# Weight chunks from 66 on behind the second stage's first rows, the first four chunks one by one, five constant products between the stages

## The chip, the cores and the metric

One core of a Trainium2 chip runs the whole program. The metric is the device time of one execution in microseconds (us). Below, PE is TensorE (matrix products), ACT is ScalarE, DVE is VectorE, POOL is GpSimd and SP is SyncE, which here only issues DMA transfers.

## What is computed

Three layers in a row. An attention with 16 heads, in which a query sees the keys of its own bucket (six sign bits of a projection); a mixture of eight experts, one for each token; and a mixture of eight experts, two for each token.

```
mask = q_bucket[:, :, :, None] == k_bucket[:, :, None, :]
scores = where(mask, scale * q @ k.T, -1e9);  attn = softmax(scores);  x = attn @ v      # 16 heads, 768 x 64
# x: 1536 tokens x 512
for e in range(8):  out[mask_e] = gate_w * (relu(x[mask_e] @ w1[e]) @ w2[e])              # first MoE, top 1
for e in range(8):  out[mask_ke] += top2_w * (relu(x[mask_ke] @ w1[e]) @ w2[e])           # second MoE, top 2
```

## The kernel before

All three layers are one program. The attention is the first stage of a plan; the two mixtures of experts are the second plan, whose experts 0 to 7 are the first MoE and 8 to 15 the second (here "first stage" is the first MoE and "second stage" the second MoE where the experts are spoken of). Each plan is an instance of `Plan` (L98): every step is added with an engine, a length, a due time and the steps that it waits for, and `order()` simulates the engines and takes, among the steps that can start soon, the one that is due first. The result is a fixed order for each engine. The tables `LENGTH`, `SHIFT`, `WAITS` (L36 to L79; with a 2 for the second plan) correct lengths and due times, and so set that order. Each engine then works through its order and waits at semaphores only for what a step reads.

Products are taken in fp32r: each fp32 operand is split into a high and a low part, and three products are added (L1130 to L1132 for the first layer of an expert, m1; L1160 to L1167 for the second). The weights of the 16 experts come in 128 chunks of 512 KB, chunk n = 8 * expert + c, c from 0 to 3 of w1 and from 4 to 7 of w2. `wload` (L246, the DMA is L257) brings a chunk into one of four `wraw` buffers, on SP's queue; `wsplit_h` (L266) makes the high part on ACT, `wsplit_l` (L272) the low part on DVE, for chunks 0 to 3 on POOL. Chunks 64 to 67 are the w1 of the second stage's first expert, chunks 68 to 71 its w2.

In the attention, the bits of a head's buckets are brought into the operand ka by a small DMA on SP, `bits_copy` (L646), and the product of ka and qa (L659) adds the mask to the scores. SP also issues the loads of each head (`loads`, L448 and L449), copies of q and k (L573, L613) and the fills with zeros of the slots in DRAM (`init_x`, L519). Chunks 0 to 3 are loaded in this stage too.

Between the experts, the rows of the second stage go through DRAM. When the first stage's expert e is done, its rows are routed: `rank_start` (L296, L298) and `rank_mm` (L304, L306) count places on PE, DVE turns the count into an index (L319, L322, tile pi), and POOL scatters the rows with four indirect DMAs (`r2_scatter`, L1276) into xs2, the slots of the second stage. `x2_load(0)` (L1306) reads the slots of the second stage's first expert back, tile xr, 104 x 4 x 512 numbers (832 KB). It waits for the scatters of experts 0 to 6. Expert 7's own rows don't take that way: PE adds them by products with one-hot matrices (`y_put`, L1263) to the transposes of the loaded rows (`x8_tr`, L1089, over `slot_start`, L806; 16 transposes), and ACT and DVE split the sum (`x_h`, `x_l`). Ahead of that, `y_h` and `y_l` (L1251, on POOL) split expert 7's result. Constant products of a zero tile wt (`warm`, L239) stand at the program's start.

The number `HOLD` (L94) names the chunk from which on ACT's split waits for the second stage's first rows to be split, and `FIRST2` the chunk whose load waits for `x2_load` to be issued; the loads stand in one line, so all later chunks follow it. The lines of the plan that the change touches are L975 (chunks 0 to 7 in the first plan), L1414 (the loads of the second), L1448 (the transposes) and L1517 (`y_l`).

Of the kernel before, what the change touches and what calls it, by code (L numbers as in the profile page):

```python
# [9 lines left out]
F32 = mybir.dt.float32  # L10
# [8 lines left out]
NB, NHEAD, S, DH = 2, 8, 768, 64  # L19
NBITS = 6  # L20
HEADS = NB * NHEAD
N, D, E, F = NB * S, NHEAD * DH, 8, 1024
# [30 lines left out]
SHIFT = {'c4': -30, 'e0t': 30, 'en1': -80, 'ene': -30, 'ex': -17.2, 'fa': 5.2, 'fo': -140, 'fr': 7, 'fs': -135,  # L53
# [4 lines left out]
WAITS = {'PE': (0, 0.0), 'ACT': (5, 0.0), 'DVE': (265, 0.0), 'POOL': (880, 0.0)}  # L58
LENGTH2 = {('POOL', 'gm', 1742): 2363, ('POOL', 'iw', 1100): 750, ('ACT', 'wh', 520): 521, ('DVE', 'wl', 600): 602, ('Q', 'wr', 2100): (2100, 1500), ('POOL', 'xm', 1023): 783,
# [6 lines left out]
    ('ACT', 'xh', 400): 403, ('DVE', 'xlo', 503): 509, ('ACT', 'xh', 745): 791, ('DVE', 'xlo', 936): 933, ('PE', 'm1', 2276): 2267, ('ACT', 'rh', 745): 761,  # L66
# [3 lines left out]
SHIFT2 = {'g1a': -95, 'g1b6': -15, 'g2a': 10.3, 'g4a': -40, 'g5a': -40, 'g5aa': -150, 'g5b6': -80, 'g9a': 15, 'gia': 20,  # L70
    'gib6': 35, 'gpa': -45, 'gva': 75, 'm1a': -7, 'm1b': 20, 'm1c': 7, 'm2a': -5, 'm2b': 14, 'm2c': 1,
    'rha': 12, 'rhb': -140, 'rla': -25, 'rlb': 25, 'sqa': -15, 'wh0a': -25, 'wh0b': 40, 'wh1a': 2, 'wh1b': -20,
    'wl0a': -35, 'wl0b': -10, 'wl0c': 45, 'wl1a': -5, 'wl1b': 35, 'wr0a': -24, 'wr0b': -18, 'wr1a': -45, 'xha': -60,
    'xhb': -20, 'xla': -25, 'xlb': -50, 'xloc': 85, 'xtb': 35, 'yc0a': -60, 'yca': -63, 'ycb': 20, 'ycc': 105,
    'yra': 5, 'yta': -2}
WAITS2 = {'PE': (0, 0.0), 'ACT': (120, 1.0), 'DVE': (0, 0.18), 'POOL': (120, 0.0)}
WAIT = 120
# [10 lines left out]
RA, K8, L1, L2, RS = 0, 7, 20, 1, 14  # L88
WP, WR, WS = 4, 30, 2.5
# [3 lines left out]
XZ, XSB = 13, 2  # L93
W0, GO, HOLD, FIRST2, WZ = 7, 300, 69, 69, -12  # L94
LONE = 30


class Plan:  # L98
# [8 lines left out]
    def add(self, name, eng, dur, fn, due, deps=(), use=(), new=(), lat=0):  # L107
        t = self.length.get((eng, name[0], dur), dur)
        dur, lat = t if isinstance(t, tuple) else (t, lat)
        due += self.shift.get(self.group(name, eng), 0)  # L110
        self.steps[name] = (eng, dur, fn, due, tuple(deps), tuple(use) + tuple(new), tuple(new), lat)
# [68 lines left out]
def lsh_attention_moe_moe2_kernel(  # L180
# [4 lines left out]
    nc = tc.nc  # L185
# [6 lines left out]
    psp = main.enter_context(tc.tile_pool(name="psp", bufs=1, space=PSUM))  # L192
# [7 lines left out]
    wt = con.tile([128, 128], F32R, name="wt")  # L200
# [285 lines left out]
    for i in range(2):  # L486
        QA.append(acon.tile([128, S], F32R, name=f"qa{i}"))
        a = acon.tile([128, S], F32R, name=f"ka{i}")
# [9 lines left out]
    en = rt.tile([E, D], F32, name="en", bufs=1)  # L498
# [300 lines left out]
    XP, XR, OH = {}, {}, {}  # L799
# [52 lines left out]
    add = plan.add  # L852
# [121 lines left out]
    for c in range(8):  # L974
        add(("wr", c), "SP", 1700, P(wload, c), (WR if c < WP else 222) + c, ([("in", 2)] if c < WP else [("in", len(inits) - 1)]) + ([("wl", c - 4, 7)] if c > 3 else []),  # L975
            lat=2500)
# [104 lines left out]
    def x_turn(key, dp):  # L1081
# [5 lines left out]
        XP[key, 2 * dp, 2] = t  # L1087

    def x8_tr(d, half):  # L1089
        if half == 0:  # L1090
            if d == 0:
                P = psp.tile([128, 2, 512], F32, name="S", bufs=2)
                XP[E, 0], XP[E, 1] = P[:, 0], P[:, 1]
            elif d > 1:
                XP[E, d] = psp.tile([128, 512], F32, name="ET", bufs=3)
        slot_start(XP[E, d], X2[0], range(2 * half, 2 * half + 2), MB, d, True)
# [327 lines left out]
    for key in range(2 * E):  # L1424
# [15 lines left out]
        for dp in range(2):  # L1440
            if key % E:
                add(("xt", key, dp), "DVE", 585 if one else 1004, P(x_turn, key, dp), z - XZ + 2 * dp,
                    [("xl", key)], use=[("xr", key)], new=[("xs", (key, dp))])
        if key == E:
            for d in range(4):
                for h in range(2):
                    k, r = 2 * d + h, [x8(d)]
                    add(("xt", E, k), "PE", 430, P(x8_tr, d, h), z - 13 + k,  # L1448
                        [("xl", E), ("yt", 7, 3) if k < K8 else ("g7", 7)] + [("xt", E, k - 1)] * (k > 0),
                        use=[("xr", E)] + r * (h == 1 or d == 1), new=r * (h == 0 and d != 1))  # L1450
        xp = pieces(key)
# [40 lines left out]
        if one:  # L1492
# [16 lines left out]
            if e == E - 1:  # L1509
                for b in range(2):  # L1510
                    add(("oh", b), "DVE", 480, P(y_ones, b), t - 1, [("g7", e)] + [("oh", 0)] * b,
                        use=[rr, ("O", ("r", e))] + [("hh", "oh")] * b, new=[] if b else [("hh", "oh")])
                    for dp in range(2):
                        y = t - .3 if dp else z + q * 14
                        ob, l = [("yo", "b")], [("ys", (-1, b, dp))]
                        add(("yh", b, dp), "ACT", 358, P(y_h, b, dp), y + .5 + .1 * b, [("yr", e, b, dp), ("yob",)], use=[tt(b, dp), mt] + ob)
                        add(("yl", b, dp), "POOL", 680, P(y_l, b, dp), y + .5 + .1 * b, [("yh", b, dp)], use=ob + [("row", e)], new=l)  # L1517
                        add(("xo", dp, b), "PE", 700, P(y_put, dp, b), t + 1 + dp + .1 * b, [("yl", b, dp), ("oh", b), ("xt", E, 4 * dp + 3)] + [("xo", dp, 0)] * b,
                            use=[x8(2 * dp), x8(2 * dp + 1), ("hh", "oh")] + ob + l)
# [196 lines left out]
```

## Time and profile before

| | |
|---|---|
| median of 3 runs | 778.31 us (776.13 to 780.4) |
| profiled execution | 780.1 us |
| its span in the trace | 778.4 us |
| PE busy | 755.1 us, 97% |
| mean granted clock of PE | 0.985 |

The span runs from the first to the last record of the trace; the profiled execution's own time is 1.7 us longer. All rows below are of this one execution. Times in the trace count from the start of the span. [...] Busy time of PE is counted by records, whatever its clock; PEld are its weight loads, which run beside the products. The DMA share is the mean busy share of the core's 16 DMA engines, GB/s what they moved. In a row of a timeline, the brackets hold the idle time before and what ended it.

### The profile page before, as it was taken

The page shows a single profiled execution, that of the slowest core. Times are in us where ns is not written, and L with a number is a line of the kernel's source. Part 1 is how long each engine was busy: PE and PEld are TensorE (multiplying, and loading weights), DVE is VectorE, ACT ScalarE, POOL GpSimd, SP SyncE. Part 2 cuts the span into 40 slices and gives each one's busy share as a digit, 9 for nine tenths or more (in the row PEclk, how much of TensorE's full clock was granted, in tenths as well). Part 3 has the DMA queues.
Part 4 walks back from the last instruction along what each step waited for, and adds up shares of the span by engine and source line. Part 5 has one row for each costly group of instructions (what it writes and reads, how often), then busy time and mean ns, then how long its engine had stood idle before and what let it go on. Part 6 is the DMA issues. An engine that isn't in the chain of part 4 may idle for free. (4 is left out here: it accounts for less than half of the span.)

```text
span 778.4 us, 14515 instructions
## 1 busy us (share of the span) xinstructions
PE 755.1 (97%) x4846; PEld 732.5 (94%) x4846; DVE 572.7 (74%) x1249; ACT 474.0 (61%) x1009; POOL 389.4 (50%) x666
## 2 busy tenths in 40 slices
PE   9989999999999999999999959999999999999996
PEld 7989999999999999999999959999999999999996
DVE  8979999999998868888888755675676566565411
ACT  7888989988888756666566643454454444344210
POOL 6434566664437531334544243028565473848384
PEclk9999999999999999999999987999999999999999
DMA  7696677887655477979896674969788585956133
GB/s 190 163 298 173 162 205 209 241 215 206 150 130 195 161 195 238 255 228 245 216 232 184 194 223 125 178 179 239 149 208 201 130 182 134 199 142 121 13 35 84
DMA packets 142114, 140.61 MB, mean 181 GB/s; under 512 B 25898, under 2 KB 122434, under 8 KB 142034
## 3 DMA queue, kind: packets, MB, share of 16 engines
q1 hardware_dynamic: 124770, 122.93, 58.6%
q0 software_dynamic: 17264, 16.69, 11.3%
q8 instruction: 40, 0.66, 0.4%
q14 instruction: 40, 0.33, 0.1%
HBM read 88.54 MB, written 34.46 MB: 158 GB/s over the span
## 5 line engine op out<-in xcount | busy, mean ns | idle before, releaser
L1353 POOL DMA_INDIRECT out_dram<-yo,idx x91 | 149.5, 1642 | 125.7 <-DVE yo L1350 100.0
L1130 PE MATMUL S<-xh,w0h 128*128 128x224 f32 (+1 forms) x512 | 162.4, 317 | 1.3 <-ACT hh L1139 0.7
L1132 PE MATMUL S<-xh,w0l 128*128 128x224 f32 (+1 forms) x512 | 160.4, 313 | 0.0
L1131 PE MATMUL S<-xl,w0h 128*128 128x224 f32 (+1 forms) x512 | 159.5, 311 | 0.0
L1139 ACT ACTIVATE hh<-S 128x448 fp32r<-128x448 f32 (+1 forms) x64 | 45.0, 704 | 113.3 <-PE S L1132 106.4
L692 DVE TENSOR_TENSOR el<-ET,eh 128x384 fp32r<-128x384 f32 x192 | 100.2, 550 | 7.7 <-ACT eh L686 5.2
L686 ACT ACTIVATE eh<-ET 128x384 fp32r<-128x384 f32 x192 | 91.0, 494 | 20.5 <-PE ET L682 20.0
L664 DVE TENSOR_REDUCE mxs<-S 128x1 f32<-128x768 f32 x96 | 91.5, 954 | 14.6 <-PE S L659 13.5
L674 ACT ACTIVATE es<-S,mxs 128x768 f32<-128x768 f32 x96 | 95.7, 997 | 7.9 <-POOL mxs L670 5.8
L1143 DVE SCALAR_TENSOR_TENSOR hh<-S,hh 128x448 fp32r<-128x448 f32 (+1 forms) x64 | 52.5, 820 | 64.1 <-ACT hh L1139 64.0
L1130 PEld LDWEIGHTS S<-xh,w0h 128*128 128x128 f32 x512 | 97.2, 190 | 1.9 <-ACT hh L1139 0.8
L272 DVE TENSOR_TENSOR w1l<-wraw,w1h 128x512 fp32r<-128x512 f32 x128 | 83.0, 683 | 21.1 <-ACT w1h L266 21.0
L1131 PEld LDWEIGHTS S<-xl,w0h 128*128 128x128 f32 x512 | 97.2, 190 | 0.8
L1132 PEld LDWEIGHTS S<-xh,w0l 128*128 128x128 f32 x512 | 97.2, 190 | 0.3
L682 PE MATMUL ET<-idf,es 128*128 128x128 f32 x576 | 91.0, 276 | 0.5 <-DVE el L692 0.4
L1167 PE MATMUL ET<-hh,w1l 128*128 128x416 f32 (+2 forms) x264 | 91.0, 345 | 0.0
L1165 PE MATMUL ET<-hh,w1h 128*128 128x416 f32 (+2 forms) x264 | 90.4, 342 | 0.0
L266 ACT ACTIVATE w1h<-wraw 128x512 fp32r<-128x512 f32 x128 | 73.5, 624 | 27.7 <-PE ET L1166 20.9
L1166 PE MATMUL ET<-hh,w1h 128*128 128x416 f32 (+2 forms) x264 | 90.1, 341 | 0.0
L266 ACT ACTIVATE w0h<-wraw 128x512 fp32r<-128x512 f32 (+1 forms) x152 | 78.2, 557 | 4.2 <-DMA wraw<-in_w1b_dram 2.6
L682 PEld LDWEIGHTS ET<-idf,es 128*128 128x128 f32 x576 | 71.7, 143 | 8.9 <-DVE el L692 2.3
L272 DVE TENSOR_TENSOR w0l<-wraw,w0h 128x512 fp32r<-128x512 f32 x120 | 77.4, 685 | 2.7 <-ACT w0h L266 1.7
(268 smaller groups left out, 1615.3 us busy)
## 6 DMA issues: line engine op xcount, KB each, us to landing
wraw<-in_w1a_dram SPq DMA_DIRECT2D x32, 512.0 KB
wraw<-in_w2a_dram SPq DMA_DIRECT2D x32, 512.0 KB
wraw<-in_w1b_dram SPq DMA_DIRECT2D x32, 512.0 KB
wraw<-in_w2b_dram SPq DMA_DIRECT2D x32, 512.0 KB
xs<-zrow SPq DMA_DIRECT2D x26, 260.5 KB
xr<-xs SPq DMA_DIRECT2D x28, 208.0 KB
qk<-in_qk_dram SPq DMA_DIRECT2D x15, 384.0 KB
xs<-zrow SPq DMA_DIRECT2D x14, 261.0 KB
```

What stands on the lines that cost most here:

```text
L266: nc.scalar.activation(wH[n][:, c], wraw[n][:, c], AF.Copy)
L272: eng.tensor_tensor(wL[n][:, c], wraw[n][:, c], wH[n][:, c], op=OP.subtract)
L664: nc.vector.tensor_reduce(MX[(3 * g + j) % 9][:, 0:1], SC[g, j][:, :, :384], axis=AX.XY, op=OP.max, negate=True)
L674: nc.scalar.activation(ES[g, j].rearrange("p (a b) -> p a b", a=2), SC[g, j][:, :, :384], AF.Exp, bias=mx[:, 2:3], scale=mx[:, 1:2], accum ...
L682: nc.tensor.transpose(T[:, j * 128:j * 128 + 128], ES[g, j][:, kb * 128:kb * 128 + 128], idf)
L686: nc.scalar.activation(EH[g, kb], ET[g, kb], AF.Copy)
L692: nc.vector.tensor_tensor(EL[g, kb], ET[g, kb], EH[g, kb], op=OP.subtract)
L1130: nc.tensor.matmul(o, wH[n][:, fs], xh, start=kd == 0, stop=False)
L1131: nc.tensor.matmul(o, wH[n][:, fs], xl, start=False, stop=False)
L1132: nc.tensor.matmul(o, wL[n][:, fs], xh, start=False, stop=kd == 3)
L1167: nc.tensor.matmul(P, wL[n][:, ws], hh, start=False, stop=f == 7)
L1353: s = nc.gpsimd.indirect_dma_start(out=out.rearrange("n (a c) -> (n a) c", a=4), out_offset=bass.IndirectOffsetOnAxis(ap=IDX[e][:, b:b + 1 ...
```

## The change

It has five parts. `HOLD` and `FIRST2` go from 69 to 66, so that chunks 66 to 68 too are issued behind the second stage's first rows. Chunk c of the first four is due 22 c after the first and waits for fill 2 + 6 c instead of fill 2. A new step `x8_warm` on PE makes five constant products of 512 columns into the tile S of the transposes, after the last y_tr of expert 7 (`("yt", 7, 3)`), and the first transpose waits for it. `y_l` of the second half waits for expert 7's routing step g5 as well. The tables of both plans are new.

```
-SHIFT = {'c4': -30, 'e0t': 30, 'en1': -80, 'ene': -30, 'ex': -17.2, 'fa': 5.2, 'fo': -140, 'fr': 7, 'fs': -135,
...
+SHIFT = {'bq': -75, 'c4': -60, 'e0t': 100, 'en': 14, 'ene': -85, 'ex': -11, 'fa': -10, 'fo': -160, 'fs': -95,
...
-W0, GO, HOLD, FIRST2, WZ = 7, 300, 69, 69, -12
+W0, GO, HOLD, FIRST2, WZ, WX = 7, 300, 66, 66, -12, 5
...
-        add(("wr", c), "SP", 1700, P(wload, c), (WR if c < WP else 222) + c, ([("in", 2)] if c < WP else [("in", len(inits) - 1)]) + ([("wl", c - 4, 7)] if c > 3 else []),
+        add(("wr", c), "SP", 1700, P(wload, c), (WR + 22 * c if c < WP else 222 + c), ([("in", 2 + 6 * c)] if c < WP else [("in", len(inits) - 1)]) + ([("wl", c - 4, 7)] if c > 3 else []),
...
+    def x8_warm(n):
+
+        P = psp.tile([128, 2, 512], F32, name="S", bufs=2)
+        XP[E, 0], XP[E, 1] = P[:, 0], P[:, 1]
+        for _ in range(n):
+            nc.tensor.matmul(P[:, 0].rearrange("p (a b) -> p a b", a=4), wt, wt[:, None].to_broadcast([128, 4, 128]),
+                             start=True, stop=True)
+
     def x8_tr(d, half):
         if half == 0:
-            if d == 0:
-                P = psp.tile([128, 2, 512], F32, name="S", bufs=2)
-                XP[E, 0], XP[E, 1] = P[:, 0], P[:, 1]
-            elif d > 1:
+            if d > 1:
                 XP[E, d] = psp.tile([128, 512], F32, name="ET", bufs=3)
...
+            add(("wx",), "PE", 250 * WX, P(x8_warm, WX), z - 13.5, [("yt", 7, 3)], new=[x8(0)])
...
-                        [("xl", E), ("yt", 7, 3) if k < K8 else ("g7", 7)] + [("xt", E, k - 1)] * (k > 0),
-                        use=[("xr", E)] + r * (h == 1 or d == 1), new=r * (h == 0 and d != 1))
+                        [("xl", E), ("yt", 7, 3) if k < K8 else ("g7", 7)] + [("xt", E, k - 1) if k else ("wx",)],
+                        use=[("xr", E)] + r * (h == 1 or d < 2), new=r * (h == 0 and d > 1))
...
-                        add(("yl", b, dp), "POOL", 680, P(y_l, b, dp), y + .5 + .1 * b, [("yh", b, dp)], use=ob + [("row", e)], new=l)
+                        add(("yl", b, dp), "POOL", 680, P(y_l, b, dp), y + .5 + .1 * b, [("yh", b, dp)] + [("g5", e)] * dp, use=ob + [("row", e)], new=l)
```

The changed program has six lines more from `x8_tr` on and one more from the tables on, so that L257 becomes L258, L646 becomes L647, L806 becomes L807 and L1306 becomes L1312.

Where the orders differ, first SP's in the attention, around the first weight chunks (xs<-zrow are fills, wraw chunks, qk and vr the next head's loads, ka<-qa the bits copy). Before:

```order
L519 DMA xs_58<-zrow 16x8x522
L257 DMA wraw<-in_w1a_dram 128x4x256 x2
L613 DMA qb<-lx 64x768
L613 DMA kb<-lx 64x768
L257 DMA wraw<-in_w1a_dram 128x4x256
L519 DMA xs_58<-zrow 16x8x522
L257 DMA wraw<-in_w1a_dram 128x4x256
L646 DMA ka_150<-qa_149 12x768
```

Now:

```order
L520 DMA xs_58<-zrow 16x8x522
L258 DMA wraw<-in_w1a_dram 128x4x256
L614 DMA qb<-lx 64x768
L614 DMA kb<-lx 64x768
L520 DMA xs_58<-zrow 16x8x522
L449 DMA qk<-in_qk_dram 128x768
L450 DMA vr<-in_v_dram 128x384
L647 DMA ka_150<-qa_149 12x768
```

One chunk stands ahead of the copy instead of four, and the next head's loads stand ahead of it, which stood behind it. Each of the three other chunks now comes alone, between two fills.

Second, SP's order where the second stage's first rows are loaded (xr<-xs). Before:

```order
L257 DMA wraw<-in_w2a_dram 128x4x256 x4
L257 DMA wraw<-in_w1b_dram 128x4x256 x4
L257 DMA wraw<-in_w2b_dram 128x4x256
L1306 DMA xr<-xs_59 104x4x512
L257 DMA wraw<-in_w2b_dram 128x4x256 x3
L257 DMA wraw<-in_w1b_dram 128x4x256
```

Now:

```order
L258 DMA wraw<-in_w2a_dram 128x4x256 x4
L258 DMA wraw<-in_w1b_dram 128x4x256 x2
L1312 DMA xr<-xs_59 104x4x512
L258 DMA wraw<-in_w1b_dram 128x4x256 x2
L258 DMA wraw<-in_w2b_dram 128x4x256 x4
L258 DMA wraw<-in_w1b_dram 128x4x256
```

The load stood behind all four chunks of w1b and one of w2b; it stands behind two chunks of w1b now.

Third, PE's order at the same place (ET<-iw,ys are the last turns of expert 7's result, S<-wt the constant products, S<-idf,xr and ET<-idf,xr the transposes of the rows, O the rank of expert 7). Before:

```order
L1214 MATMUL ET<-iw,ys 112x144 x2
L296 MATMUL O<-carry,onr 112x16
L298 MATMUL O<-pen,idr 112x16
L806 MATMUL S<-idf,xr 128x104 x8
L806 MATMUL ET<-idf,xr 128x104 x6
L304 MATMUL O<-hot,onr 112x8
L306 MATMUL O<-hot,upr 112x16
L806 MATMUL ET<-idf,xr 128x104 x2
L1263 MATMUL S<-hh,yo 128x416 x2
```

Now:

```order
L1220 MATMUL ET<-iw,ys 112x144 x2
L1095 MATMUL S<-wt 128x512 x5
L297 MATMUL O<-carry,onr 112x16
L299 MATMUL O<-pen,idr 112x16
L807 MATMUL S<-idf,xr 128x104 x8
L807 MATMUL ET<-idf,xr 128x104 x2
L305 MATMUL O<-hot,onr 112x8
L307 MATMUL O<-hot,upr 112x16
L807 MATMUL ET<-idf,xr 128x104 x6
L1269 MATMUL S<-hh,yo 128x416 x2
```

The five products stand between the last turns and the transposes, and expert 7's rank comes four transposes earlier. Expert 6's rank (L304, L306 before; L305, L307 now), on which its scatters hang, has moved as well: of the 96 first-layer products of expert 7 (L1130 to L1132), 72 stood ahead of it and 24 behind; now 48 stand ahead and 48 behind.

## Rows read from the trace of the kernel before

**Rows 1.** Busy time, share of the span and instructions of each engine.

```profile
PE 755.1 (97%) x4846; PEld 732.5 (94%) x4846; DVE 572.7 (74%) x1249; ACT 474.0 (61%) x1009; POOL 389.4 (50%) x666
```

**Rows 2.** Windows: stretch, us, busy us (instructions) PE, PEld, DVE, ACT, POOL; clock, DMA share, GB/s.

```profile
58.17:257.00 198.83, 197.62 (x1350) 188.52 (x1349) 181.96 (x347) 176.84 (x415) 111.16 (x316) 1.00 0.71 187
257.00:457.60 200.60, 197.63 (x1535) 191.93 (x1533) 164.95 (x507) 123.82 (x284) 81.81 (x151) 1.00 0.77 221
...
478.01:770.80 292.79, 292.79 (x1600) 290.33 (x1598) 169.40 (x262) 120.60 (x201) 160.97 (x105) 1.00 0.67 150
770.80:778.40 7.60, 0.17 (x2) 0.00 (x0) 0.48 (x1) 0.00 (x0) 2.00 (x2) 0.77 0.30 87
```

**Rows 3.** The same windows in the attention stage.

```profile
51.33:53.61 2.28, 0.01 (x1) 0.03 (x1) 0.39 (x1) 1.94 (x7) 0.85 (x2) 1.00 0.97 283
54.76:58.17 3.41, 3.41 (x15) 3.22 (x15) 1.81 (x3) 1.68 (x3) 1.53 (x4) 0.51 0.95 287
```

**Rows 4.** Timeline of SP's queue: start us, us, engine, line, operation, count.

```profile
37.99 1.85 SPq L257 DMA_DIRECT2D wraw<-in_w1a_dram  x2
...
42.71 0.60 SPq L257 DMA_DIRECT2D wraw<-in_w1a_dram  x1
...
44.08 1.75 SPq L257 DMA_DIRECT2D wraw<-in_w1a_dram  x1
45.93 0.81 SPq L646 DMA_DIRECT2D ka<-qa  x1
```

**Rows 5.** Timeline of PE, with the idle time before and its releaser.

```profile
53.61 0.59 PE L659 MATMUL S<-ka,qa 96*128 96x384 f32 x2 [2.28 <-ACT w0h L266]
```

**Rows 6.** The windows again, around the change of stages.

```profile
457.60:460.95 3.35, 0.10 (x1) 0.00 (x1) 2.50 (x9) 1.78 (x6) 1.45 (x2) 0.99 0.54 116
460.95:465.37 4.42, 0.00 (x0) 0.00 (x0) 1.31 (x11) 1.26 (x3) 0.00 (x0) 0.50 0.98 218
465.37:472.60 7.23, 7.23 (x35) 7.23 (x35) 0.67 (x2) 0.00 (x0) 0.00 (x0) 0.50 0.03 10
472.60:478.01 5.41, 5.41 (x18) 5.16 (x18) 3.60 (x12) 1.44 (x3) 3.09 (x3) 0.50 0.39 110
```

**Rows 7.** Timeline of SP's queue around the change of stages.

```profile
444.98 4.65 SPq L257 DMA_DIRECT2D wraw<-in_w1b_dram  x4
451.25 0.37 SPq L257 DMA_DIRECT2D wraw<-in_w2b_dram  x1
457.90 0.34 SPq L1306 DMA_DIRECT2D xr<-xs  x1
458.67 22.13 SPq L257 DMA_DIRECT2D wraw<-in_w2b_dram  x3
```

**Rows 8.** Timeline of POOL: expert 6's four scatters.

```profile
443.98 3.03 POOL L1276 DMA_INDIRECT xs<-row,pi  x1 [2.63 <-ACT w1h L266]
...
451.44 0.94 POOL L1276 DMA_INDIRECT xs<-row,pi  x1 [0.31 <-issue]
```

**Rows 9.** Line L1276, 443 to 453.5: those scatters from issue to landing.

```profile
DMA to landing us min/median/max: 6.4/6.5/8.6
```

**Rows 10.** Line L1276, 473 to 480: expert 7's scatters from issue to landing.

```profile
DMA to landing us min/median/max: 3.5/3.6/4.2
```

**Rows 11.** Timeline of PE: the 24 products ahead of expert 6's rank, first of them, and it.

```profile
438.79 0.28 PE L1130 MATMUL S<-xh,w0h 128*128 128x224 f32 x1
...
441.47 0.17 PE L304 MATMUL O<-hot,onr 112*112 112x8 f32 x1
```

**Rows 12.** Timeline of PE: constant products at the program's start.

```profile
9.89 1.99 PE L239 MATMUL ET<-wt 128*128 128x512 f32 x8
```

**Rows 13.** Line L806 before 400: transposes of expert 0's rows; ns min/median/max.

```profile
L806 PE MATMUL S<-idf,x x8: 261/275/275, 257.8 to 258.6; 112*128 112x112 f32 x8
```

**Rows 14.** Timelines of SP's queue and of PE: a later bits copy and its product.

```profile
64.67 0.80 SPq L646 DMA_DIRECT2D ka<-qa  x1
...
70.00 0.60 PE L659 MATMUL S<-ka,qa 96*128 96x384 f32 x2
```

More of the change, by code (lines that the diff above doesn't have):

```diff
@@ L52 @@
     ('POOL', 'xb', 956): 915, ('DVE', 'oh', 330): 311, ('PE', 'xo', 650): 670}
-SHIFT = {'c4': -30, 'e0t': 30, 'en1': -80, 'ene': -30, 'ex': -17.2, 'fa': 5.2, 'fo': -140, 'fr': 7, 'fs': -135,
[4 rows of a table removed]
-WAITS = {'PE': (0, 0.0), 'ACT': (5, 0.0), 'DVE': (265, 0.0), 'POOL': (880, 0.0)}
+SHIFT = {'bq': -75, 'c4': -60, 'e0t': 100, 'en': 14, 'ene': -85, 'ex': -11, 'fa': -10, 'fo': -160, 'fs': -95,
[5 rows of a table added]
+WAITS = {'PE': (0, 0.0), 'ACT': (95, 0.2), 'DVE': (35, 0.53), 'POOL': (1120, 0.0)}
 LENGTH2 = {('POOL', 'gm', 1742): 2363, ('POOL', 'iw', 1100): 750, ('ACT', 'wh', 520): 521, ('DVE', 'wl', 600): 602, ('Q', 'wr', 2100): (2100, 1500), ('POOL', 'xm', 1023): 783,
@@ L63 @@
     ('PE', 'g6', 114): 105, ('PE', 'g7', 116): 105, ('DVE', 'gi', 383): 439, ('ACT', 'g8', 110): 126, ('DVE', 'gp', 331): 323, ('DVE', 'g9', 700): 698,
[2 rows of a table removed]
-    ('ACT', 'xh', 400): 403, ('DVE', 'xlo', 503): 509, ('ACT', 'xh', 745): 791, ('DVE', 'xlo', 936): 933, ('PE', 'm1', 2276): 2267, ('ACT', 'rh', 745): 761,
[3 rows of a table removed]
[L70 to L76, printed above, removed]
[2 rows of a table added]
+    ('DVE', 'xm', 150): 105, ('PE', 'xt', 430): 224, ('ACT', 'xh', 400): 403, ('DVE', 'xlo', 503): 509, ('ACT', 'xh', 745): 791, ('DVE', 'xlo', 936): 933,
[3 rows of a table added]
+SHIFT2 = {'g1a': -170, 'g2a': -15, 'g2b6': -95, 'g4a': -35, 'g5a': 1.3, 'g5aa': -230, 'g8a': -15, 'g9a': 26, 'gia': 23,
+    'gib6': -120, 'gpa': -15, 'm1a': -13, 'm1b': 16, 'm1d': 5, 'm2a': -8, 'm2b': 19, 'm2c': 8, 'rha': -45,
+    'rhb': -170, 'rla': -25, 'rlb': 60, 'rlc': -65, 'rld': -65, 'sqa': -17, 'wh0a': -20, 'wh1a': -15, 'wh1b': -115,
+    'wl0a': -33, 'wl0b': 60, 'wl0c': 35, 'wl0d': -120, 'wl1a': -18, 'wl1b': 78, 'wl1c': 20, 'wl1d': -60, 'wr0a': -15,
+    'wr0b': -20, 'wr1a': -30, 'wr1b': -35, 'xla': -20, 'xlb': -125, 'xloa': -120, 'xlob': -85, 'xloc': 75, 'xmc': 50,
+    'xmd': -120, 'xta': -20, 'xtc': -40, 'yc0b': -55, 'yca': -10, 'yra': -5, 'yta': -2, 'ywd': -15}
+WAITS2 = {'PE': (120, 0.0), 'ACT': (120, 0.5), 'DVE': (0, 0.01), 'POOL': (120, 0.0)}
 WAIT = 120
```

19 rows, old and new, of tables (LENGTH2, SHIFT) are left out of this document.

## The prediction

> **What bounds the kernel now.** I read the busy times first: TensorE (PE) is busy for 97% of the span and the next engine, VectorE (DVE), for 74% [rows 1]. So the end moves only by what PE idles, or runs at the lower clock. Then the windows: PE stands still for 1.2 us between 58.17 and 257.00, for 3.0 us between 257.00 and 457.60, and not at all between 478.01 and 770.80; from there to the end it is 7.6 us [rows 2]. A microsecond won before 478.01 therefore reaches the end whole. Two places are left.
>
> The first is in the attention stage. PE stands still from 51.33 to 53.61 and then runs at a granted clock of 0.51 until 58.17 [rows 3]. What it waits for is the product of ka and qa [rows 5], which reads the bits that SP's bits copy brings over. That copy was issued at 45.93, behind four weight chunks and their neighbours in SP's queue [rows 4], while the DMA share was 0.97. The row names ACT's split of w0h as releaser, but that product reads nothing of w0h; I take the copy to be the one that came last.
>
> The second is the change from the first MoE to the second. [...] The rows' load (xr<-xs) was issued at 457.90, after the last scatter into xs, issued at 451.44 [rows 7, 8], had landed, 6.4 us after its issue [rows 9]. While it landed, five chunks (512 KB each) were on their way [rows 7]. With little traffic the same scatter lands in 3.5 us [rows 10].
>
> The sum is made against the profiled execution's own 780.1 us; the median of the runs is 778.3, 1.8 below. A measurement here tells about 0.5% (3.9 us) from no change: faster means under 774.4, slower over 782.2.
>
> **Chunks 0 to 3 one by one.** In the changed order a single chunk stands between two fills and the bits copy where there were four; the next come 22 plan units later each. If the copy no longer queues, the 2.28 us go, and so does the cause of the low clock: 3.41 us at half are 1.7 us lost. That is 4.0 us. Bounds: 0, where another wait takes its place, to -4.0. I take -4.0, since rows 3 show the queue full there and nowhere later in this stage does PE idle for over 1.2 us in all. The splits of these chunks stand on ACT and POOL by the same table; chunk 0 is needed only by the first MoE at about 257, so a later split costs nothing.
>
> **Rows ahead of chunks 66 to 68.** SP now has the rows' load behind two of expert 0's w1b chunks, where it had five chunks of the second stage ahead. Two things follow. Expert 6's rank product comes 24 first-stage products earlier on PE (48 of expert 7's 96 stand ahead instead of 72); 24 of them take 441.47 - 438.79 = 2.7 us [rows 11], and DVE's index step and POOL's four scatters follow it. And the last scatter, with two chunks beside it and not five, lands closer to 3.6 than to 6.4 us: 2.8 us. Together 465.37 - 5.5 = 459.9 for the first transpose. Bounds: -2.8, where only one of the two holds, to -6.6, where the first transpose follows the end of PE's other work at 458.8 (two parts below). I take -5.5.
>
> Chunks 66 and on then come later. Behind the rows each needs 0.524 MB / 218 GB/s = 2.4 us [rows 6]. Chunk 66 is thus there 2.4 us after the rows. PE needs it only after transposes and row products (12.6 us, rows 6) and the 48 products of chunks 64 and 65 (0.18 us each by rows 2, 292.79 / 1600): 21 us after the rows, so some 18 are left for its split. Cost 0; without that cover the first product of chunk 66 would wait. Each of w2b's chunks is needed later still.
>
> **Five constant products.** Eight 128x512 products take 1.99 us at the start of the program [rows 12]; five take 1.2, from 457.6 to 458.8, where PE has nothing else to do. Cost 0. If the rows had landed by 457.6, they would cost 1.2.
>
> **The clock.** From 465.37 to 478.01 PE works for 12.64 us at 0.50 [rows 6]; at the full clock, where the same kind of transposition takes 0.27 us and not its double [rows 13], it would save half, 6.3 us. In the trace the clock was still 0.99 in the first 3.35 us of the idle time and fell after them; the idle time is 7.77 us in all, and would now be 459.9 - 458.8 = 1.1 us. That speaks for the full saving. Against it: 7.23 us of transposes, with PE busy throughout, did not raise the clock, nor did the 5.41 us behind them. So the transposes themselves may let it fall somewhere in the middle of those 12.6 us. I take -2.0, a third; bounds 0 to -6.3. [...]
>
> **The wait of y_l, and the tables.** y_l now also waits for a routing step, but POOL's order keeps four y_l steps and then the scatters: 0. The new tables move 778 lines of PE's order, 401 of ACT's, 554 of DVE's. Both MoE stages leave PE 3.0 and 0 us of idle time [rows 2], so there is nothing much to win and I take 0; what they could cost stands under rival D.
>
> **Sum:** -4.0 - 5.5 - 2.0 = -11.5; 780.1 - 11.5 = 768.6, and on the median 778.3 - 11.5 = 766.8. I forecast **767 us**.
>
> **The rivals.**
> A, the clock holds throughout. The short idle time speaks for it, the 12.6 us of busy PE that didn't raise the clock against it. -4.0 - 5.5 - 6.3 = -15.8: 762.5.
>
> B, only the landing or only the rank gets earlier, and the clock stays at half: -4.0 - 2.8 = -6.8: 771.5. For it: the scatters' own starts take 7.5 us [rows 8] and wait on POOL for whatever stands ahead.
>
> C, the chunks now behind the rows' load share the DMA engines with it. Three more chunks are 7.2 us at 218 GB/s [rows 6], which would eat what the earlier issue gains: -11.5 + 7.2 = -4.3: 774.0, no change. Against it: in the trace before, chunks were issued behind the rows' load too (at 458.67, [rows 7]), and PE went on 7.5 us after the issue, about what 0.85 MB at 218 GB/s (3.9 us) and a landing of 3.6 us make together. [...]
>
> D, slower: in the changed order the next head's two loads (384 and 192 KB) stand ahead of each head's bits copy, where they stood behind it. 0.59 MB at 287 GB/s [rows 3] are 2.05 us. In the trace before a copy is issued at 64.67 and its product starts at 70.00 [rows 14]: 5.3 us in which the copy must land, less where the tables move the product forward. If the 2.05 us lie open on 14 heads, that is +28.7 - 11.5: 795.5. It decides from 11.5 / 14 = 0.8 us a head. Against it: 5.3 us is much against a copy of 37 KB, and the copy itself waits for DVE's bits, so the loads may well be issued in that wait.
>
> **How the numbers follow.** Forecast 0.47, A 0.12, B 0.18, C 0.14, D 0.09. Faster is forecast, A and B: 0.77; the same is C: 0.14; slower is D: 0.09. The range: from 762, A's time, to 777, one above C with half of its first term gone (776.0). It leaves out D and little else; the forecast's own range, by its bounds, is 763 to 772.
>
> **What the profile after would show.** Right: no idle time of PE over 0.5 us before the ka,qa product between 40 and 60, and a clock of 1.0 there; the rows' load issued at about 448.4 (457.90 less 5.5 and less the first term's 4.0); the last scatter before it landing in under 4.5 us; the first transpose about 1 us behind the fifth constant product; a clock over 0.5 in part of the stretch between the first transpose and the first product of the second MoE. Wrong: a gap of over 4 us before the transposes (then B or C: B where the issue is late, C where issue to start is over 7.5 us), or gaps before the ka,qa products of many heads (D). The clock term is wrong if the whole stretch stands at 0.50 or at 1.0.

## The result and the profile after

The changed kernel takes **765.75 us** (median of 4 runs, 764.64 to 765.91) against 778.17 us (4 runs, 776.13 to 780.4): a ratio of 0.9833, 95% interval 0.9814 to 0.9851. Forecast was 767. Measured again (e5 below) it was 769.75 us, ratio 0.9866 (0.9830 to 0.9903). Both lie in the range and under the 774.4 from which the prediction speaks of faster. The profiled execution took 765.78, its span is 764.0 us, against 780.1 and 778.4.

Busy time, which answers to [rows 1]. PE is busy for 98% instead of 97%:

```profile
PE 748.8 (98%) x4851; PEld 726.9 (95%) x4851; DVE 569.5 (75%) x1249; ACT 471.1 (62%) x1009; POOL 390.8 (51%) x666
```

SP's queue at the change of stages, the change's counterpart to [rows 7]. The rows' load (xr<-xs) is issued at 447.71, ahead of six chunks, where it came at 457.90:

```profile
447.71 0.35 SPq L1312 DMA_DIRECT2D xr<-xs  x1
448.16 1.21 SPq L258 DMA_DIRECT2D wraw<-in_w1b_dram  x2
449.46 16.72 SPq L258 DMA_DIRECT2D wraw<-in_w2b_dram  x4
```

POOL's last scatter of expert 6, and the landing of the four (compare [rows 8, 9]); the load follows the last one by 4.2 us, where it took 6.5:

```profile
443.47 0.94 POOL L1282 DMA_INDIRECT xs<-row,pi  x1 [0.31 <-issue]
```

```profile
DMA to landing us min/median/max: 4.2/6.0/7.2
```

PE at that place, with its idle time and releaser in brackets. L1220 are the last turns of expert 7, L1095 the five products, L807 the transposes. The first line is the kernel before's, where the transposes waited 7.68 us:

```profile
465.37 3.75 PE L806 MATMUL S<-idf,xr 104*128 104x104 f32 x16 [7.68 <-DMA xr<-xs]
```

```profile
452.11 0.74 PE L1220 MATMUL ET<-iw,ys 128*112 128x144 f32 x4 [0.45 <-ACT ys L1196]
452.59 1.42 PE L1095 MATMUL S<-wt 128*128 128x512 f32 x5
...
454.75 2.03 PE L807 MATMUL S<-idf,xr 104*128 104x104 f32 x16 [0.63 <-DMA xr<-xs]
```

Windows (stretch, us, busy us and count of PE, PEld, DVE, ACT, POOL, granted clock as a share of PE's full speed, DMA share, GB/s). The first lies where the attention lost its time [rows 3]; the third is the stretch from the first transpose to the first product of expert 8, which took 12.8 us at 0.50 [rows 6]; the last two answer to [rows 2]:

```profile
48.00:54.00 6.00, 6.00 (x46) 5.86 (x45) 5.02 (x10) 5.02 (x13) 3.53 (x10) 1.00 0.85 209
452.59:454.75 2.16, 1.53 (x10) 1.21 (x9) 1.21 (x6) 1.63 (x6) 0.28 (x1) 1.00 1.08 231
454.75:461.66 6.91, 6.91 (x50) 6.89 (x51) 4.65 (x23) 1.51 (x5) 2.78 (x4) 1.00 0.83 261
461.66:755.86 294.20, 293.12 (x1598) 290.02 (x1598) 171.51 (x266) 122.30 (x204) 162.32 (x107) 1.00 0.67 150
755.86:764.00 8.14, 0.28 (x3) 0.05 (x1) 0.56 (x2) 0.00 (x0) 2.34 (x3) 0.83 0.31 89
```

Last, a wait that was not there before, in expert 8's second layer, and DVE beside it. PE waits for hh, and hh stands on DVE behind idx (L1325), which waits for a DMA of xm, the numbers that go with the rows; SP issues it at 476.77, behind the next expert's rows:

```profile
485.08 0.46 PE L1172 MATMUL ET<-hh,w1h 128*128 128x416 f32 x1 [1.08 <-DVE hh L1149]
```

```profile
482.66 0.23 DVE L1325 TENSOR_SCALAR idx<-xm,quarter 128x13 int32<-128x13 f32 x1 [3.64 <-DMA xm<-xs]
482.81 1.29 DVE L273 TENSOR_TENSOR w1l<-wraw,w1h 128x512 fp32r<-128x512 f32 x2
484.01 1.02 DVE L1149 SCALAR_TENSOR_TENSOR hh<-S,hh 128x832 fp32r<-128x832 f32 x1
```

To compare runs I divide each profiled execution at four marks that every trace has: the first transpose of the first MoE (L806 or its successor), expert 7's last turns, the first transpose of the second stage, and the first product of expert 8. The stretches between them, in us, worked out from those starts and the span, for these two and all experiments. (The kernel before's first product of expert 8 starts at 478.16, so its fourth stretch is 12.79 and not the 12.64 up to 478.01 of the prediction.)

| profiled execution | attention | first MoE | idle and products | transposes and row products | to the end | span |
|---|---|---|---|---|---|---|
| before | 257.8 | 199.0 | 8.53 | 12.79 | 300.2 | 778.4 |
| changed | 253.0 | 199.1 | 2.64 | 6.91 | 302.3 | 764.0 |
| e1 before, 36 products | 254.2 | 199.3 | 9.01 | 7.23 | 300.1 | 769.8 |
| e2 before, 5 products | 254.2 | 199.2 | 8.20 | 12.59 | 300.1 | 774.3 |
| e3 before, rows first | 254.4 | 200.6 | 4.76 | 12.59 | 300.1 | 772.5 |
| e4 changed, no products | 253.2 | 200.6 | 2.28 | 7.27 | 301.4 | 764.8 |
| e5 changed, again | 253.3 | 200.3 | 3.30 | 10.09 | 301.6 | 768.5 |
| e6 before, one by one | 256.7 | 201.4 | 9.11 | 11.77 | 300.8 | 779.9 |
| e7 changed, four at once | 253.9 | 201.5 | 3.20 | 6.90 | 302.0 | 767.5 |
| e8 changed, rows later | 253.0 | 201.2 | 5.02 | 11.69 | 300.0 | 770.9 |
| e9 changed, old tables | 255.9 | 198.9 | 4.88 | 12.92 | 299.9 | 772.6 |
| e10 idx moved | 253.2 | 200.0 | 3.21 | 6.91 | 300.9 | 764.2 |
| e11 products between | 253.0 | 200.2 | 3.05 | 8.28 | 301.2 | 765.8 |
| e12 eight products | 253.0 | 203.1 | 3.11 | 6.90 | 300.7 | 766.8 |

So the 14.4 us of the two profiled executions are -4.8 in the attention, +0.1 in the first MoE, -5.9 of idle time, -5.9 from the clock and +2.1 behind it. The first MoE's stretch runs from 198.9 to 203.1 us over all traces, with no pattern by edit; what spreads it is not shown, and a difference of 2 us between two medians can't be put on a stage by one trace each.

### The profile page after: what moved, and what is told of

It is laid out like the page before. It is cut to its first block, busy times and chain, and to the rows that moved or that the text cites. A ratio compares the mean times of both kernels' runs of the same rounds, so it can differ in the third digit from the quotient of the medians.

```text
span 764.0 us, 14517 instructions
## 1 busy us (share of the span) xinstructions
PE 748.8 (98%) x4851; PEld 726.9 (95%) x4851; DVE 569.5 (75%) x1249; ACT 471.1 (62%) x1009; POOL 390.8 (51%) x666
## 3 DMA queue, kind: packets, MB, share of 16 engines
q0 software_dynamic: 17264, 16.69, 11.5%
## 5 line engine op out<-in xcount | busy, mean ns | idle before, releaser
L1149 DVE SCALAR_TENSOR_TENSOR hh<-S,hh 128x448 fp32r<-128x448 f32 (+1 forms) x64 | 52.5, 820 | 52.7 <-ACT hh L1145 52.5
L1172 PE MATMUL ET<-hh,w1h 128*128 128x416 f32 (+2 forms) x264 | 90.2, 342 | 1.1 <-DVE hh L1149 1.1
```

## The experiments

My theory after the result: the rows come earlier by the early rank and the free queue, the short idle time keeps the clock up, and the attention's wait is gone. The rival that the traces left open: that the products, the tables or chance did one or the other. All times are medians of interleaved runs with the kernel before on the same chip (778.2 us beside e1 to e4, 779.2 beside e5 to e8, 778.4 beside e9 to e11, 779.0 beside e12); each of these four groups ran on a chip of its own.

The granted clock in the last column is the mean over a whole execution. It counts the program's end, where the clock falls too (0.77 in the last 7.60 us before [rows 2], 0.83 in the changed kernel's last 8.14). The profiled executions whose transposes and row products took 6.90 to 8.28 us (changed, e1, e4, e7, e10 to e12) show a mean of 0.996 to 0.999, those where they took 10.09 to 12.92 us 0.985 to 0.994; so 0.996 or more is read below as a clock that held up to the end.

| run | us, median (range) | ratio to before (95%) | granted clock of the runs |
|---|---|---|---|
| e1 | 775.76 (771.43 to 780.64) | 0.9980 (0.9952 to 1.0007) | 0.992 to 0.998 |
| e2 | 778.19 (775.99 to 785.76) | 1.0015 (0.9989 to 1.0042) | 0.983 to 0.989 |
| e3 | 774.23 (771.50 to 777.58) | 0.9954 (0.9931 to 0.9977) | 0.986 to 0.991 |
| e4 | 770.63 (766.64 to 772.02) | 0.9907 (0.9872 to 0.9942) | 0.991 to 0.993, one 0.998 |
| e5 | 769.75 (765.11 to 772.93) | 0.9866 (0.9830 to 0.9903) | 0.994 to 0.999 |
| e6 | 780.47 (778.94 to 784.16) | 1.0017 (0.9998 to 1.0037) | 0.984 to 0.988 |
| e7 | 769.40 (768.10 to 772.60) | 0.9881 (0.9851 to 0.9911) | 0.996 to 0.998 |
| e8 | 773.76 (771.28 to 776.55) | 0.9925 (0.9901 to 0.9950) | 0.988 to 0.993 |
| e9 | 775.32 (771.44 to 778.07) | 0.9961 (0.9943 to 0.9979) | 0.987 to 0.993 |
| e10 | 763.63 (762.47 to 765.94) | 0.9812 (0.9794 to 0.9831) | 0.997 to 0.998 |
| e11 | 766.41 (765.61 to 767.53) | 0.9850 (0.9832 to 0.9868) | 0.997 to 0.999 |
| e12 | 766.55 (765.75 to 768.56) | 0.9824 (0.9801 to 0.9848) | 0.996 to 0.998 |

**The clock alone: e1 and e2.** The kernel before with `x8_warm` and nothing else moved, 36 products in e1 and five in e2:

```
-W0, GO, HOLD, FIRST2, WZ = 7, 300, 69, 69, -12
+W0, GO, HOLD, FIRST2, WZ, WX = 7, 300, 69, 69, -12, 36
```

> The kernel before with one edit: 36 constant products (some 7.7 us at the full clock) between expert 7's last turns and the second stage's first transposes, where PE idles for 7.68 us; nothing else moves. It tells the clock's share from the share of the earlier rows. Theory (the idle time alone makes the clock fall, and transposes keep a clock that is up): the rows land as late as before, but the stretch from the first transpose to the first product of expert 8 shrinks from 12.8 to about 6.9 us at a clock of 1.0; 5.9 us faster, about 772. Rival (the transposes themselves let the clock fall): that stretch falls to 0.50 in its middle, 2 us faster at most, 776 or more.

> The kernel before with one edit: the five constant products alone (1.2 us), rows as late as before. Theory: some 6.5 us of idle time are left behind them, the clock falls all the same, the stretch from first transpose to first product stays at 12.8 us: no change, 778. Rival (a few products just behind the last turns are enough): 5.9 us faster, 772.

Timeline of PE in e1, then a window of e1 up to the first product of expert 8, and windows of e2, whose last ends 0.36 us ahead of that product:

```profile
453.99 8.46 PE L1094 MATMUL S<-wt 128*128 128x512 f32 x36
...
462.51 2.03 PE L806 MATMUL S<-idf,xr 104*128 104x104 f32 x16
```

```profile
462.51:469.74 7.23, 7.16 (x52) 6.95 (x51) 3.33 (x11) 1.32 (x3) 1.21 (x2) 1.00 0.02 5
```

```profile
455.30:460.19 4.89, 0.11 (x2) 0.02 (x1) 3.26 (x16) 2.38 (x7) 1.44 (x2) 1.00 0.90 194
460.19:461.61 1.42, 0.01 (x1) 0.01 (x1) 0.00 (x0) 0.00 (x0) 0.00 (x0) 0.50 0.88 231
461.61:473.84 12.23, 12.23 (x49) 12.00 (x50) 3.87 (x12) 1.44 (x3) 2.88 (x3) 0.50 0.17 50
```

With the wait filled, the transposes ran at 1.00 and their stretch took 7.23 us, with the rows no earlier; the 36 products took 8.46 us, where some 7.7 had been expected. With five products and 6.20 us of idle time behind them the clock fell ahead of the transposes, and the time did not change: five products far from the rows won nothing. But e1's median gained 2.5 us and not 5.9, and its interval takes in no change. Its granted clocks go down to 0.992, and where it fell in those runs, in the attention as in [rows 3] or amid the transposes, was not seen: one profiled execution shows only that the clock can hold. Nor is the clock the whole of what is missing: the five runs of e1 at 0.996 or more took 771.4 to 777.0 us (median 775.6), the seven below 773.5 to 780.6 (median 775.9). So e1 shows what a held clock does to this stretch in one trace, and not that it is worth 5.9 us in the median.

**The rows alone: e3.** HOLD and FIRST2 at 66 in the kernel before; PE's order is the same to the last row.

> The kernel before with one edit: HOLD and FIRST2 at 66, so that the rows' load stands behind two chunks; PE's order, and so expert 6's rank, stays where it is. Theory: the last scatter lands up to 2.8 us sooner after its issue, the first transpose comes as much earlier, and with some 5 us of idle time left the clock still falls: 2.8 us faster, 775.5. Rival (chunks beside the scatters don't set their landing): no change, 778. If the clock holds as well: 8.7 us faster, 769.6.

```profile
452.87 0.34 SPq L1306 DMA_DIRECT2D xr<-xs  x1
```

```profile
449.63 0.94 POOL L1276 DMA_INDIRECT xs<-row,pi  x1 [0.30 <-issue]
```

```profile
455.80:459.80 4.00, 0.09 (x2) 0.00 (x1) 3.09 (x13) 1.77 (x6) 1.45 (x2) 0.82 1.05 223
459.80:472.03 12.23, 12.23 (x49) 12.00 (x50) 3.40 (x18) 1.14 (x3) 2.88 (x3) 0.50 0.54 172
```

(The last window ends 0.36 us ahead of expert 8's first product.) The load followed the last scatter by 3.2 us instead of 6.5. Over all traces this gap is 6.4 to 7.0 us where four or five chunks of w1b and w2b stand ahead (before, e1, e2, e6, e8) and 3.2 to 4.8 where two do. The clock still fell, and 4.0 us (0.9931 to 0.9977 of before) are what theory gave and a little more.

**Without the products: e4.** WX = 0 in the changed kernel.

> The changed kernel without the five constant products; nothing else moves. Theory (the products keep the clock, as without them PE would idle for 2.6 us of the 3 us before the transposes): the clock falls to 0.50 for the stretch from the first transpose to the first product of expert 8, 5.9 us slower, about 771.6. Rival (the rows come early enough by themselves): the clock stays at 1.0 and the time at 765.7.

Window of e4 from the first transpose to the first product of expert 8:

```profile
456.09:463.36 7.27, 7.18 (x51) 6.99 (x51) 4.97 (x24) 1.87 (x5) 3.07 (x4) 1.00 0.79 250
```

The profiled execution kept its clock (7.27 us for the transposes at 1.00, 1.43 us of idle time ahead) and took 766.64. The five other runs show 0.991 to 0.993 and 768.8 to 772.0 us. So the rows' early landing can be enough, but seldom was. The changed kernel as it is shows 0.996 or more in 6 of 10 runs (the first four and e5); with e7 and e10 to e12, which have five or more products, it is 27 of 31, without products one of 6. But e4's and e5's intervals overlap, and most of the runs that held the clock are of other variants on other chips. That five products hold it more often is likely, and not shown.

**The changed kernel again, and its parts undone: e5 to e8.**

> The changed kernel as it is, for its spread and as the neighbour of the next three on the same chip. Theory (the transfers' queue in the attention and the clock at the change of stages are what made the kernel before vary): median 765.7, all runs within 2 us, granted clock 0.997 or 0.998 in each, where the kernel before spreads over 7 us. Rival (four runs were too few to see it): a spread as wide as before's.

Windows of e5 around the transposes, which began at 456.84, 1.30 us after the last product:

```profile
456.84:458.70 1.86, 1.86 (x16) 1.86 (x17) 1.72 (x12) 0.11 (x1) 0.51 (x1) 0.99 1.10 349
458.70:465.53 6.83, 6.83 (x29) 6.70 (x29) 2.10 (x11) 0.11 (x1) 2.67 (x3) 0.50 0.65 203
465.53:466.93 1.40, 1.40 (x9) 1.39 (x8) 0.38 (x1) 0.93 (x2) 1.10 (x2) 1.00 0.54 167
```

This miss mattered most. The transposes started at the full clock, it fell in their middle, while PE was busy throughout, and rose again under the row products: 10.09 us instead of 6.91. That is the case that the prediction had forecast. Four of the six runs show 0.994 or 0.995 and 769.3 to 772.9 us, two 0.998 or more and 765.1 and 767.0. In e7, with the same order at this place and 3.20 us from the last turns to the transposes (3.30 in e5), it did not fall.

For e6 (the kernel before) and e7 (the changed one) only this line was exchanged, in e6 as shown and in e7 the other way round:

```
-        add(("wr", c), "SP", 1700, P(wload, c), (WR if c < WP else 222) + c, ([("in", 2)] if c < WP else ...
+        add(("wr", c), "SP", 1700, P(wload, c), (WR + 22 * c if c < WP else 222 + c), ([("in", 2 + 6 * c)] if c < WP else ...
```

> The kernel before with one edit: chunks 0 to 3 one by one; the second plan's order stays. Theory (the bits copy no longer queues behind four chunks): no wait of PE for the ka,qa product over 0.7 us before 60; where a run of the kernel before lost the 2.3 us of wait and the 1.7 us of clock it gains 4.0, where it lost under 1 it gains that; median 1 to 4 us faster, 775.5, with a narrower spread. Rival (the copy was late for another reason): the wait stays, no change.

> The changed kernel with one part undone: chunks 0 to 3 issued together again, behind one fill; only SP's order moves. Theory: the bits copy behind them waits as in the kernel before, 0 to 2.3 us from run to run, in some runs with a fall of the clock: median 1 to 4 us slower, about 767.5, spread over 4 us or more. Rival (the new tables alone protect the copy): 765.7 and a spread under 2 us.

What PE waited for in e6 between 20 and 257 us (in all, times, longest), then the first ka,qa product of e7 that waited:

```profile
PE ET L682 <- DVE el L692: 2.6, 3, 1.6
PE S L659 <- ACT es L674: 0.7, 1, 0.7
```

```profile
52.21 0.59 PE L660 MATMUL S<-ka,qa 96*128 96x384 f32 x2 [0.15 <-DMA ka<-qa]
```

In e6 the wait for the copy is gone, and with the old tables 2.6 us of waits for DVE's el (the low part of the transposed attention weights) stand in its place: the attention ends at 256.7, later than the 254.2 to 254.4 of e1 to e3, which have the order of before. The forecast of 775.5 missed: the median is 780.5, no change. In e7 the copy, with four chunks ahead but the new tables, costs 0.15 us there. A second wait for it, of 0.75 us at 156.65, doesn't tell: e4, with the chunks one by one, waits 0.56 us at 156.05. The attention ends 0.6 to 0.9 us later than in the other runs with the new order, and the median is that of e5. So one by one is not what the attention gains from by itself; with the new tables it is worth under 1 us of the attention. What it is worth in the whole time stays open: the clock held in all six runs of e7 (768.1 to 772.6 us) and in two of e5 only (765.1 and 767.0), and these two lie below all six.

> The changed kernel with one part undone: HOLD and FIRST2 at 69, so that the rows' load stands behind four chunks again; expert 6's rank keeps its early place. Theory (the chunks beside the scatters set their landing): the last scatter lands some 2.5 us later after its issue, the idle time before the transposes grows by as much, the five products no longer keep the clock: 2.5 + up to 5.9, so 768 to 774, likeliest 772. Rival (the early rank alone is enough): 765.7.

POOL's last scatter, the rows' load and the first transposes in e8:

```profile
445.52 0.94 POOL L1282 DMA_INDIRECT xs<-row,pi  x1 [0.30 <-issue]
```

```profile
452.28 0.34 SPq L1312 DMA_DIRECT2D xr<-xs  x1
```

```profile
459.18 3.09 PE L807 MATMUL S<-idf,xr 104*128 104x104 f32 x16 [3.02 <-DMA xr<-xs]
```

In e8 (HOLD and FIRST2 at 69) the load follows the last scatter by 6.8 us again, the stretch before the transposes is 5.02 us and the clock falls (the 16 transposes take 3.09 us, where they take 2.03 at 1.00; the stretch is 11.69): the median is 4.0 us above e5's on the same chip. The early rank alone is not enough.

**The tables: e9.**

> The changed kernel with the tables of before: HOLD, FIRST2, the chunks one by one, the products and the wait of y_l are in, only SHIFT, WAITS, LENGTH2, SHIFT2 and WAITS2 are old. Theory (the tables carry the attention's part and the early rank): the attention ends as late as with the chunks one by one alone (last turns of expert 7 at 457 to 458, a wait on el in place of the one on the bits), expert 6's rank comes 2.7 us later than in the changed kernel, some 4 us of idle time are left before the transposes and the clock falls: 775 to 777. Rival (the tables are worth nothing, as predicted): 766 to 770.

The same three in e9:

```profile
449.47 0.94 POOL L1281 DMA_INDIRECT xs<-row,pi  x1 [0.30 <-issue]
```

```profile
452.65 0.35 SPq L1311 DMA_DIRECT2D xr<-xs  x1
```

```profile
459.75 3.74 PE L806 MATMUL S<-idf,xr 104*128 104x104 f32 x16 [2.88 <-DMA xr<-xs]
```

Landing is as quick as in e3 (3.2 us from last scatter to load), but the scatter comes 5.4 us ahead of the last turns, as in every run with the old tables, and not 8.4 to 8.7 as with the new ones. The stretch before the transposes is 4.88 us, the clock falls (the 16 transposes take 3.74 us, as before at 0.50; the stretch is 12.92), and the attention ends at 255.9. Without the tables the change is worth 3.1 us, about what the earlier rows alone won in e3 (4.0).

**A better version: e10, e11, e12.** In e10 idx waits for the relu that it stood ahead of:

```
-            add(("xm", key), "DVE", 150, P(x2_meta, e), z - 12 + (0 if e else 20), [("xl", key) if e else ("xl2",)], use=[("xm", e)], new=[("ix", e)])
+            add(("xm", key), "DVE", 150, P(x2_meta, e), z - 12 + (0 if e else 20), [("xl", key) if e else ("xl2",)] + [("rl", E, 3)] * (key == E), use=[("xm", e)], new=[("ix", e)])
```

> The changed kernel with one step moved: DVE's step that makes idx of the second stage's first expert, which waits for a DMA of xm, stands behind the fourth relu of that expert (hh) instead of ahead of it. Theory (PE's new wait of 1.1 us in expert 8's second layer is this hh, queued on DVE behind idx): that wait is gone, the time from the first product of expert 8 to the end falls from about 302 to 301 us or less; 1.1 us faster than the changed kernel with the same clock, 765 to 769 by the run. Rival (hh is late by itself or the next step waits instead): no change.

DVE of e10 at that place; hh (L1149) now runs ahead of idx (L1325), and PE's wait at L1172 is gone:

```profile
482.96 1.02 DVE L1149 SCALAR_TENSOR_TENSOR hh<-S,hh 128x832 fp32r<-128x832 f32 x1 [1.72 <-ACT hh L1145]
484.55 0.23 DVE L1325 TENSOR_SCALAR idx<-xm,quarter 128x13 int32<-128x13 f32 x1 [0.56 <-DMA xm<-xs]
```

From the first product of expert 8 to the end it takes 300.9 us, where the changed kernel, e4, e5 and e7 took 301.4 to 302.3; these four traces all have the wait for hh at L1172 (1.1 to 1.2 us), and e10 to e12 have none. At 763.63 us it is below both kernels, though the changed kernel did not run beside it; the 1 us is shown by the trace, the rest of the distance to 765.75 and 769.75 is not.

> The kernel of the run with idx moved, and with eight constant products ahead of the transposes instead of five and two more ahead of each later group of eight transposes. Theory (transposes alone keep PE busy but let the clock fall in some runs; 128x512 products among them hold it): the clock stays at 1.0 from the first transpose to the first product of expert 8 in every run, that stretch takes 6.9 + 1.3 = 8.2 us, the granted clock is 0.997 or more in all runs and the spread within 3 us; median about 766. Rival (the fall comes from the idle time ahead or from elsewhere): clocks of 0.994 in half of the runs as in the changed kernel, median 770.

> The kernel with idx moved, and eight constant products instead of five, none between the transposes. Theory (a shorter idle time ahead of the transposes makes the clock safer, at no cost, as PE waits for the rows there anyway): the idle time before the transposes falls from 1.2 to about 0.6 us, the granted clock is 0.997 or more in all runs, the first transpose comes when the rows land, median 763 to 766. Rival (the clock falls from the transposes themselves): granted clocks of 0.994 in some runs, as in the changed kernel when it ran again, median 767 or more.

e11 adds three products ahead of the transposes and six among them, e12 only the three. The clock held in all ten runs, as it did in all five of e10 beside e11, so the products among the transposes showed nothing but their price: 8.28 us for the stretch instead of 6.91, and 2.8 us in the median, of which the stretch accounts for 1.4. In e12 the rows had 0.42 us to come behind the last product. Its median of 766.55 lies a little above the 763 to 766 expected. Its ratio and e10's overlap (0.9824 and 0.9812), and that eight products hold the clock more surely than five is not shown: with idx moved, five held it in all five runs too. The first MoE took 203.1 us in its profiled execution, which the edit doesn't touch.

## Why the prediction was right, and where it was not

The time (767 forecast, 765.75 and 769.75 measured), the sign and the place were right. The terms were not all, and that their sum came out is in part luck. By the traces the terms are -1.2, -5.9, -5.9 and +2.1 where the clock held: -10.9, beside the -11.5 forecast. A first term that was 2.8 too large made up for most of a clock term that was 3.9 too small, and a cost of 2.1 was left out. With e5's clock (-2.7) the sum is -7.7. Measured were -12.4 and -9.5; the remaining 1.5 to 1.8 us are not explained, and the first MoE alone varies by more.

**Chunks 0 to 3 one by one (-4.0).** In the profiled pair it was -4.8, but this is the step that was mis-sized: I took one execution's wait for the kernel's. That the copy is what PE waits for there was right: e2's trace names it (0.9 us, DMA ka<-qa). Three more executions with the attention in the order of before (e1, e2, e3) waited 0.9 us at most ahead of that product, without a fall of the clock, and ended the attention at 254.2 to 254.4; the changed order ends it at 253.0 to 253.3. Typically the term is worth 1.2 us, and that together with the new tables. The mean clocks hint the same: 19 of the 74 runs of the kernel before beside the experiments show 0.985 or less, as its profiled execution does, though a mean doesn't tell where the clock fell. I had said that the profiled execution lay 1.8 us above the median and not asked which term held them. The edit alone (e6) is worth nothing: what the prediction named for its bound of 0, another wait in its place, came true there, on el.

**Rows ahead of chunks 66 to 68 (-5.5).** Right in size (-5.9) and in both halves: the last scatter comes 3.2 us earlier against the last turns (2.7 forecast; e9 shows that the tables carry it), and the load follows it 2.2 us sooner (2.8 forecast; e3 and e8 show that the chunks ahead carry it). Rival C fell: with four chunks issued behind it while it was under way (one before), the rows' load took 7.0 us from issue to first transpose, 7.5 before, and 6.9 to 7.5 in all traces but e1, where the products ahead were still running.

**Five products (0).** Their price was right (1.2 us forecast, 1.42 from the first one's start to the last one's end). That I gave them no gain was probably wrong: without them e4 loses the clock in 5 of 6 runs, with them the same kernel loses it in 4 of 10. That is too few runs to show it.

**The clock (-2.0).** In the profiled execution it was -5.9: rival A, and by the sign that the prediction had set (the whole stretch at 1.0) the term was wrong there. Over the runs it is in between, and not by the mechanism that A named alone: e5 shows the fall amid the transposes on which the -2.0 rested (12.79 to 10.09 us, -2.7). Both happen to the same program. At half the clock I had taken one transposition for double the 0.27 us of [rows 13]; by the records it takes 0.42 us there (median of L806 from 465 on, before) and 0.275 at 1.00 (L807, changed). It is the 16 together that take nearly the double, 3.75 and 2.03 us.

**Chunks 66 and on later (0), the tables (0).** The chunks were in time; what came late was a neighbour that I did not follow. With expert 8's first product some 12 us earlier behind expert 7's last turns, xm came too late for idx, and hh was queued behind it on DVE: 1.1 us, of the 2.1 that the rest of the program got longer; another 0.5 lie in the last stretch (8.14 us, 7.60 before). The tables I costed at zero, for want of idle time to win. e9 puts them at 6 to 9 us of the change's worth (3.1 us beside the kernel before without them, 9.5 and 12.4 with them): they carry the early rank, and with them the attention ends 2.6 to 2.9 us sooner.

**Rival D** fell: no trace with the changed order shows its 0.8 us a head. In the changed kernel all waits of L660 are 1.1 us, none of them put down to the copy; the longest waits for a copy in the other traces with that order are 0.56 us in e4 and 0.75 in e7, each at one head.

## What to carry to other kernels

A wait read from one execution is a sample (the one before the ka,qa product was 2.28 us in one trace and at most 0.9 in three others): where DMA traffic sets it, read it in several traces before it goes into a sum, above all if that execution is slower than the median. A gain at a junction has two halves, what is late (here a scatter's landing behind weight chunks) and what the wait does to the clock behind it; filling the wait with constant products saved the second half here only where they left at most 1.3 us of idle time ahead of the awaited work, and not each time then (e5); with 2.9 to 6.2 us of it (e2, e8, e9) the clock fell. And whatever comes earlier overtakes something on an engine that works in order (here hh stood behind idx on DVE, and PE waited 1.08 us for it): look for steps there that wait for a transfer which did not come earlier too.

## What the runs showed of the hardware

That the clock can fall while PE is busy with transposes: in e5 it fell from 1.00 to 0.50 at 458.70, with PE's records showing it busy since 456.84, and came back at 465.53 under the row products. Whether the transposes or the 1.30 us of idle time ahead of them made it fall is not shown. The rows at half speed before [rows 6] had shown only that 7.23 us of transposes, and 5.41 us of row products behind them, didn't raise it. Beside identical orders at this place and 3.30 and 3.20 us of preceding stretch, it fell in e5 and not in e7, so the same order gives stretches 3 us apart (10.09 and 6.90); what sets the one or the other no run shows.

And how long an indirect scatter takes to land depends on the loads ahead of it, by a factor of two where that alone was changed: from the last scatter's issue to the load that waits for it 3.2 us with two chunks ahead (e3) and 6.5 with five (before). Over all traces it is 3.2 to 4.8 us with two, 6.4 to 7.0 with four or five.
